# Edge masks of a sliding-window attention kernel, built by few wide operations ahead of all else

## The chip, the cores and the metric

One core of a Trainium2 chip runs the whole program. The metric is the device time of one execution in microseconds (us). TensorE appears in the profile as PE (matmuls) and PEld (weight loads), VectorE as DVE, ScalarE as ACT, GpSimd as POOL, and the queue that issues most DMAs as SP.

## The reference, cut to what matters

```python
# x: 2048 x 512, 32 heads of 16, window 256
mod = (silu(c) @ w_mod)                      # six vectors sa, ca, ga, sb, cb, gb
h = layernorm(x) * (1 + ca) + sa
q, k, v = split(h @ wqkv)                    # (cut)
mask = (i - j >= 0) & (i - j < 256)
o = softmax(where(mask, q @ k.T * Dh**-0.5, -1e9)) @ v
x = x + ga * (o @ wo)
# then a second layernorm and an MLP over tokens (cut)
```

The attention is banded. In the first four of eight stretches of rows, the blocks at the edges of the band are masked by adding a large negative number to the scores inside PSUM.

## The kernel before: the parts that matter

A mask is added by a matmul: a selector (edge_w, an identity for one half of the columns of each parity) times a triangle of zeros and -32768 (edge_t or edge_n). All three tensors are constants that GpSimd builds once.

```python
def emit_edges():                            # GpSimd throughout
    po.memset(tri4[:], 1.0)
    po.affine_select(out=tri4[:], ...)       # (cut) a triangle for each 32 rows
    po.memset(edge_w[:], 0.0)
    po.memset(edge_n[:], NEG)
    for q in range(4):
        rows = slice(32 * q, 32 * q + 32)
        po.tensor_copy(out=tri[rows, :], in_=tri4[rows, q, :])
        for a in range(2):
            for par in range(2):
                po.tensor_copy(out=edge_w[rows, a, par, a, :], in_=identity[rows, rows])
    for m in range(4):
        for diag, (a, b) in enumerate(((NEG, 0.0), (-NEG, NEG))):
            for dst in (edge_t[:, diag, m, :], edge_n[:, diag, m, diag, :]):
                po.tensor_scalar(out=dst, in0=tri[:], scalar1=a, scalar2=b, op0=ALU.mult, op1=ALU.add)
```

They are used in the scores of each stretch that adds its mask:

```python
te.matmul(dst, lhsT=edge_w[rows, a, :, :, :], rhs=neg, start=False, stop=True, ...)  # neg: edge_n or edge_t
```

Ahead of the first scores lies a start-up in which each engine works through a fixed list. PE's list opens with warm-up matmuls on zeros, whose result is not used:

```python
WARM = 24
def e_warm(e):
    te.matmul(box["warm"][:], lhsT=zt[:, 0:P], rhs=zt[:], start=True, stop=True)
# PE's order: 14 warm, transpose of silu, 2 warm, 32 small products with wmod (ps_fm),
#             transposes of x (psb), qkb, projections (pq), first scores
# DVE's order: statistics of x0, em, reciprocal, statistics of x1, silu, nm, sT, two normalizations (xn), ...
# GpSimd's order: clear a part of VT, emit_edges, clear a part of VT, split k into KT, ...
```

The softmax here doesn't subtract the row's maximum and nothing guards it: scores larger than these inputs give would overflow.

## Time and profile before

| | before |
|---|---|
| median (3 runs) | 267.24 us |
| span in the profile | 264.8 us |
| PE / DVE / ACT / GpSimd busy | 94 / 73 / 70 / 36% |
| masks complete / first read | 10.5 / 16.75 us |
| first statistics of x (DVE) | 2.86 us |
| silu ready / its transpose starts (PE) | 5.85 / 6.42 us |
| first scores | 16.63 us |

### The profile page before, as it was taken

The page shows a single profiled execution, that of the slowest core. Times are in us where ns is not written, and L with a number is a line of the kernel's source. Part 1 is how long each engine was busy: PE and PEld are TensorE (multiplying, and loading weights), DVE is VectorE, ACT ScalarE, POOL GpSimd, SP SyncE. Part 2 cuts the span into 40 slices and gives each one's busy share as a digit, 9 for nine tenths or more (in the row PEclk, how much of TensorE's full clock was granted, in tenths as well). Part 3 has the DMA queues.
Part 4 walks back from the last instruction along what each step waited for, and adds up shares of the span by engine and source line. Part 5 has one row for each costly group of instructions (what it writes and reads, how often), then busy time and mean ns, then how long its engine had stood idle before and what let it go on. Part 6 is the DMA issues. An engine that isn't in the chain of part 4 may idle for free.

```text
span 264.8 us, 10695 instructions
## 1 busy us (share of the span) xinstructions
PE 248.2 (94%) x4769; PEld 136.8 (52%) x4769; DVE 193.5 (73%) x435; ACT 185.4 (70%) x268; POOL 95.9 (36%) x182
## 2 busy tenths in 40 slices
PE   7898999999998988899999999999999999999993
PEld 2576667656556654455544454445444444444441
DVE  5778896777847359999948888999998730415875
ACT  3479999999999899999999999999416431000000
POOL 8755321495289945553893031440000000000000
PEclk9999999999999999999999999999999999999999
DMA  7995400000017000000014862020499800001122
GB/s 212 369 382 197 42 5 6 2 5 2 2 49 196 5 4 5 2 2 2 5 38 128 227 172 85 2 61 23 152 362 397 360 2 0 21 0 63 59 99 79
DMA packets 31599, 25.35 MB, mean 96 GB/s; under 512 B 6076, under 2 KB 29632, under 8 KB 31552
## 3 DMA queue, kind: packets, MB, share of 16 engines
q1 hardware_dynamic: 31544, 24.66, 29.5%
q8 instruction: 37, 0.61, 0.9%
q14 instruction: 10, 0.08, 0.1%
q10 hardware_dynamic: 8, 0.00, 0.0%
HBM read 22.55 MB, written 2.10 MB: 93 GB/s over the span
## 4 chain that ended last, share of the span: by engine, by line
PE 67%; ACT 19%; DVE 8%; issue 4%; POOL 0%; ACTq 0%; POOLq 0%
PE pu L194 32%; ACT et L194 15%; PE pxy L194 13%; PE psa L194 8%; PE pq L194 5%; PE pa L194 4%; PE pv L194 3%; ACT lz L194 3%; DVE st L194 2%; DVE VT L194 1%; PE pt L194 1%; DVE part L194 1%; DVE OT L194 1%; PE psb L194 1%; DVE h L194 1%
## 5 line engine op out<-in xcount | busy, mean ns | idle before, releaser
L194 ACT ACTIVATE et<-psa 128x1536 bf16<-128x1536 f32 x75 | 109.1, 1455 | 4.0 <-PE psa L194 2.1
L194 PE MATMUL pu<-hb,w1p 128*128 128x512 bf16 x224 | 53.1, 380 | 0.8 <-DVE part L194 0.8
L194 PE MATMUL pu<-guT,w 128*128 128x512 bf16 x224 | 49.0, 379 | 0.0
L194 ACT ACTIVATE et<-psb 128x512 bf16<-128x512 f32 x75 | 45.1, 601 | 0.0
L194 PE MATMUL pxy<-et,ones_bd 128*32 128x192 bf16 (+3 forms) x960 | 38.7, 233 | 0.9 <-issue 0.9
L194 PE MATMUL pxy<-et,VT 128*32 128x192 bf16 (+3 forms) x960 | 38.4, 234 | 0.9 <-DVE OT L194 0.5
L194 PEld LDWEIGHTS <-w 128*128 128x128 bf16 x224 | 21.9, 98 | 26.4
L194 PE MATMUL psa<-QT,KT 32*128 32x192 bf16 (+3 forms) x720 | 29.8, 230 | 5.6 <-ACT et L194 4.9
L194 PEld LDWEIGHTS <-w1p 128*128 128x128 bf16 x224 | 20.3, 98 | 25.5 <-issue 2.3
L194 POOL TENSOR_SCALAR KT<-kb,mask_par 128x512 bf16<-128x512 bf16 (+1 forms) x36 | 22.9, 645 | 25.9 <-DVE kb L194 22.2
L194 PE MATMUL pq<-h1T,wqkv 128*128 128x512 bf16 (+1 forms) x128 | 30.1, 355 | 0.3 <-ACT VT L194 0.3
L194 PEld LDWEIGHTS <-KT 32*128 32x128 bf16 x960 | 16.1, 92 | 26.2 <-issue 23.9
L194 PEld LDWEIGHTS <-VT 128*32 128x32 bf16 x960 | 23.6, 96 | 11.6 <-issue 10.1
L194 PE MATMUL psb<-QT,KT 32*128 32x192 bf16 (+3 forms) x240 | 29.3, 231 | 0.0
L194 DVE SCALAR_TENSOR_TENSOR o<-pu,b2FM,bc_all 128x512 f32<-128x512 f32 x16 | 11.6, 748 | 20.2 <-PE pu L194 20.0
L194 DVE TENSOR_TENSOR et<-et,maskt 128x512 bf16<-128x512 bf16 (+2 forms) x56 | 24.9, 480 | 0.6 <-ACT et L194 0.5
L194 PEld LDWEIGHTS <-ones_bd 128*32 128x32 bf16 x960 | 23.2, 97 | 1.2 <-issue 1.1
L194 DVE BATCH_NORM_STATS2 st<-x 128x6 f32<-128x512 bf16 x32 | 21.7, 680 | 1.3 <-DMA x<-in_A_x_dram 1.1
L194 DVE TENSOR_TENSOR OT<-pxy,lz 128x256 bf16<-128x256 f32 x32 | 13.4, 420 | 10.6 <-ACT lz L194 10.1
L194 PEld LDWEIGHTS <-wqkv 128*128 128x128 bf16 x192 | 14.0, 97 | 13.4 <-issue 4.8
L194 PE MATMUL pv<-wqkv,h1T 128*32 128x256 bf16 x512 | 17.9, 274 | 0.2 <-DVE VT L194 0.2
L194 PE MATMUL pa<-wod,OT 128*128 128x512 bf16 x64 | 17.3, 381 | 0.3 <-ACT part L194 0.3
(113 smaller groups left out, 358.2 us busy)
## 6 DMA issues: line engine op xcount, KB each, us to landing
w1p<-in_B_w_dram SPq DMA_DIRECT2D x14, 512.0 KB, 6.1
w<-in_B_w_dram SPq DMA_DIRECT2D x14, 512.0 KB, 8.4
wmod<-in_w_mod_dram SPq DMA_DIRECT2D x6, 512.0 KB, 5.5
x<-in_A_x_dram SPq DMA_DIRECT2D x16, 128.0 KB, 4.8
out_dram<-otile SPq DMA_DIRECT2D x16, 128.0 KB, 1.7
wqkv<-in_A_wqkv_dram SPq DMA_DIRECT2D x2, 384.0 KB, 5.4
wqkv<-in_A_wqkv_dram SPq DMA_DIRECT2D x1, 512.0 KB, 5.0
wod<-in_A_wo_dram SPq DMA_DIRECT2D x1, 512.0 KB, 8.4
```

Source lines behind the costliest of these rows:

```text
L194: ins = call(*args, **kwargs)
```

## The change

The intent is to build the masks sooner and with fewer instructions. The selector moves to DVE, one copy for both parities; the triangles are written for four blocks by one GpSimd operation; both go to the head of the lists.

```diff
+    def emit_edge_w():
+        ve.memset(edge_w[:], 0.0)
+        for q in range(4):
+            rows = slice(32 * q, 32 * q + 32)
+            for a in range(2):
+                ve.tensor_copy(out=edge_w[rows, a, :, a, :], in_=identity[rows, rows].unsqueeze(1).to_broadcast([32, 2, 32]))
...
-        po.memset(edge_w[:], 0.0)
...
-            for a in range(2):
-                for par in range(2):
-                    po.tensor_copy(out=edge_w[rows, a, par, a, :], in_=identity[rows, rows])
-        for m in range(4):
-            for diag, (a, b) in enumerate(((NEG, 0.0), (-NEG, NEG))):
-                for dst in (edge_t[:, diag, m, :], edge_n[:, diag, m, diag, :]):
-                    po.tensor_scalar(out=dst, in0=tri[:], ...)
+        tris = tri[:].unsqueeze(1).to_broadcast([P, 4, 32])
+        for diag, (a, b) in ((1, (-NEG, NEG)), (0, (NEG, 0.0))):
+            for dst in (edge_t[:, diag, :, :], edge_n[:, diag, :, diag, :]):
+                po.tensor_scalar(out=dst, in0=tris, ...)
```

The long list of the emission order is renumbered, and the two entries of the masks stand first in it. Nothing else moves.

## The prediction

> **What bounds the kernel now.** I read the page first, to see which engine is full and when. Part 1 gives each engine's busy time, its share of the span and its instructions:
>
> ```profile
> PE 248.2 (94%) x4769; PEld 136.8 (52%) x4769; DVE 193.5 (73%) x435; ACT 185.4 (70%) x268; POOL 95.9 (36%) x182
> ```
>
> PE is busy for 94% of the 264.8 us; GpSimd, from which the change takes work, for 36%. An engine that is a third busy can still hold up one moment, so the second question is who reads the three mask tensors (edge_w, edge_n, edge_t), and when. I asked the view by tile for edge_w in the first 20 us; its columns are shortest, median and longest duration in ns, then the first and last start:
>
> ```profile
> L194 PEld LDWEIGHTS <-edge_w x24: 92/93/93, 16.8 to 19.2; 32*128 32x128 bf16 x24
> L194 POOL COPY edge_w<-identity x16: 199/202/376, 4.0 to 7.1; 32x32 bf16<-32x32 bf16 x16
> ...
> who waited for it (us, times):
> ```
>
> GpSimd writes the selector between 4.0 and 7.5 us, PE loads it first at 16.75, and the list of those who waited for it is empty. The lists of edge_n and edge_t are empty too. The timeline of GpSimd shows the last write and what follows (start, duration, group, and in brackets the idle time before it):
>
> ```profile
> 10.28 0.21 POOL L194 TENSOR_SCALAR edge_n<-tri 128x32 bf16<-128x32 bf16 x1
> 10.43 0.95 POOL L194 MEMSET VT<- 128x1024 bf16 x1
> 14.95 1.39 POOL L194 TENSOR_SCALAR KT<-kb,mask_par 128x256 bf16<-128x256 bf16 x3 [3.57 <-ACT kb L194]
> ```
>
> The masks are complete at 10.49, 6.3 us before anyone wants them, and behind them GpSimd clears a block of VT and then waits 3.57 us for ACT's kb. So GpSimd's long build is off the path twice over.
>
> The third view is the chain of waits in order of time, over the first 17 us (start, duration, what):
>
> ```profile
> 1.33 5.16 PE pxy L194 x14
> 6.49 0.10 PE st_ps L194
> 6.60 0.54 PE pxy L194 x2
> 7.13 0.93 PE ps_fm L194 x32
> 8.06 0.47 PE psb L194 x8
> ```
>
> It runs over the warm-up matmuls (pxy), the small transpose of silu, the modulation products and the transposes of x, and later over DVE's statistics, KT, the projections and pv. GpSimd is nowhere in it before the first scores at 16.6.
>
> The last view is DVE's timeline, because the change puts new work there:
>
> ```profile
> 1.67 0.06 DVE L396 MEMSET bc_m<- 32x1 f32 x1
> 2.86 0.69 DVE L194 BATCH_NORM_STATS2 st<-x 128x6 f32<-128x512 bf16 x1 [1.13 <-DMA x<-in_A_x_dram]
> 3.59 0.18 DVE L194 BATCH_NORM_AGGREGATE mv<-st 128x2 f32<-128x6 f32 x1
> 3.69 0.25 DVE L194 TENSOR_SCALAR em<-em 4x128 f32<-4x128 f32 x1
> ...
> 5.60 0.25 DVE L194 TENSOR_TENSOR silu<-c,rm 4x128 bf16<-4x128 bf16 x1
> ```
>
> DVE sits idle for 1.13 us until the first block of x lands, then works without a gap until 5.97. The new work goes just into that hole.
>
> **What the Trainium skill says.** "VectorE: DVE Perf Modes", in its section on the TRN2 errata, counts an operation from SBUF to SBUF as 58 cycles at 0.96 GHz plus the elements over the mode's rate, and adds that a single operation was measured with about 150 fixed cycles. For a copy of 64 bf16 elements at four per cycle that is (58 + 16) / 0.96 = 77 ns, or (150 + 16) / 0.96 = 173 ns. The trace agrees with both in its way: DVE's copy of 4 elements to sT lasts 160 ns, but independent short operations start 100 ns apart (3.59 and 3.69 above), so their ends overlap. The same page, under "Zero memsets can be issued as uint32 (trn2)", says that clearing in 4-byte words halves the elements; the trace shows DVE clearing 512 bf16 of zt as 256 uint32 in 0.27 us, and the compiled new kernel shows edge_w cleared as 128 words.
>
> "SBUF — State Buffer", section "SBUF: two separate sides", says that DVE in a two-port mode and GpSimd take a shared port pair as an exclusive lock, the later one blocked for the other's whole instruction. The trace agrees for GpSimd: its slowest edge_w copy took 376 ns against a median of 202 while DVE normalized. In the other direction I see little: that DVE operation took 0.41 us, the median of its group being 0.406.
>
> **The change part by part.** Comparing the two compiled programs engine by engine: apart from renumbering, the emission order is the same, with two entries taken to the front. PE and ACT run the same instructions in the same order.
>
> Removed from GpSimd: the clearing of edge_w (from 3.09 to the next start at 3.34: 0.25 us); 16 copies of 32x32 into it (3.81 to 7.60 is 3.79 us for these and the four copies of tri; the first tri copy takes 3.96 - 3.81 = 0.15 to the next start, so 3.79 - 4 x 0.15 = 3.19 us); and 16 small triangle operations in 10.43 - 7.60 = 2.83 us.
>
> Added to GpSimd: four triangle operations of 128x128. From rows of the same operation, 128x32 takes 211 ns and 128x256 at least 473 ns, so 128x128 is an estimated 211 + 96 x (473 - 211) / 224 = 323 ns, less an overlap of 35 ns that the small ones show (211 ns long, 175 ns apart): 4 x 0.288 = 1.15 us. Net: -0.25 - 3.19 - 2.83 + 1.15 = **-5.1 us of GpSimd**. The build shrinks from 10.43 - 2.55 = 7.88 to about 2.8 us; it also moves ahead of the first clearing of VT, from 2.55 to about 1.66, and ends near 4.4. The two clearings of VT follow until about 6.3, and GpSimd then waits for ACT's kb about 8.6 us instead of 3.57. None of the 5.1 us is on the path: **0 us gained**.
>
> Added to DVE, between 1.67 and the first statistics: one clearing of 128 words (half of zt's 0.27, so 0.14 us) and eight copies of 32x64. The clearing can start near 1.70 and the first copy, which depends on it, near 1.88. At 100 to 130 ns from start to start (the 100 of above plus some for the elements: the copy to sT_rep moves 128 elements and lasts 217 ns, 57 more than that of 4 elements) the eight need 0.8 to 1.04 us and are through between 2.68 and 2.92. The first block of x lands at 2.86. So the statistics begin **0 to 0.1 us late**. If the copies did not overlap at all, at 190 ns each, they would end at 3.40 and the delay would be 0.54 us.
>
> What a delay costs: silu is ready at 5.85 and its transpose begins at 6.42. The list of waits puts 0.42 us of PE's loading there down to DVE, but the chain puts the warm-up matmuls there up to 6.49, and DVE had finished silu half a microsecond before. I choose the chain: about 0.5 us of slack. The other branch is the normalization of x at 6.71: ACT's rs is ready at 6.24, again 0.4 to 0.5 us early. A delay of 0.1 us vanishes in either, and one of 0.54 would leave about 0.1 us. Sum: **0 us, with at most a few tenths lost**. I take 267.2 us.
>
> **Rivals.** First: the lock bites DVE. GpSimd will be working without a gap from 1.66 to 6.3, and each of the eight copies may have to wait for a GpSimd operation of 0.2 to 0.5 us. Then the copies end at 1.88 + 8 x 0.2 = 3.5 or later, the statistics start 0.6 us or more late, and the time goes up by 0.1 to 0.5 us, to 267.3 to 267.7. For it: the lock as the skill tells it. Against it: the normalization above, which ran among GpSimd copies at its usual length.
>
> Second: a quieter GpSimd helps DVE. From 6.3 to 10.5 us the port pair is now free, where before some 25 GpSimd operations ran. DVE's work from 9.2 to 12.5 is on the chain, so any nanosecond saved counts. But the statistics there take 0.68 us, as at 14.12 and 14.89 (0.64 and 0.66), where few or none ran. I give it 0.1 to 0.2 us, to 267.0.
>
> Third: masks that are ready earlier let the first scores start earlier. They wait for projections and KT, and PE reaches them right behind the pq matmuls, so no: 0 us. A shift of some tenths at the start may also change which wait ends last in the crowded schedule behind it, by tenths in either direction.
>
> **Range and chances.** The three runs of before lie within 0.3 us. Together with the rivals (-0.3 to +0.5 us) I put the 8-in-10 range at 266.6 to 267.9. Two per cent would be 5.3 us, more than all GpSimd work removed, none of which is on the path, and far more than the DVE work added: 0.98 for within 2%, 0.01 for either side.
>
> **What would show each step.** Right: GpSimd busy near 90.8 us and DVE near 194.5; the last write of edge_t or edge_n ends near 4.4; GpSimd's wait for ACT's kb grows to about 8.6 us; the first statistics start by 3.0; silu's transpose stays near 6.4 and the first scores near 16.6. Wrong: first statistics at 3.3 or later, or single copies much longer than 0.2 us (first rival); first scores earlier than 16.4 with shorter DVE rows between 9 and 12.5 (second rival); or both kernels alike up to 20 us and apart later, which nothing here foresees.

## More of the kernel before

One more view than the prediction shows matters for the result: the timeline of PE's weight loads of before, as start, duration, group and, in brackets, the idle time before it.

```profile
4.72 0.15 PEld L194 LDWEIGHTS <-zt 128*128 128x128 bf16 x1 [0.28 <-issue]
5.15 0.15 PEld L194 LDWEIGHTS <-zt 128*128 128x128 bf16 x1 [0.27 <-issue]
5.47 0.53 PEld L194 LDWEIGHTS <-zt 128*128 128x128 bf16 x3 [0.17 <-issue]
6.42 0.09 PEld L194 LDWEIGHTS <-silu 4*128 4x128 bf16 x1 [0.42 <-DVE nm L194]
```

Each warm-up matmul has one load. Up to 5.15 the loads come 0.43 us apart, then three come within 0.53 us: PE changes to about twice its pace near 5.4. The row of the granted clock reads 9 tenths or more in every slice, the first too, and does not show this; the distance of the loads does. The clock records in the trace, from which that row is made, agree with the loads: the first of them begins at 5.34 us, at full clock, and the row counts the time ahead of it as full too.

## The result, and the profile after

The changed kernel took 267.37 us (median of 4 runs, 266.91 to 267.52), the kernel before 267.37 us with a fourth run added. A ratio in this document is the mean time of one kernel's runs over that of the other's of the same rounds, so not quite the ratio of the medians. Here it is 0.9997, with a 95% interval of 0.9979 to 1.0014. The time lies in the predicted range. The profile, however, did not do what the prediction said. Part 1 of the page after:

```profile
PE 248.8 (94%) x4769; PEld 136.8 (52%) x4769; DVE 195.5 (74%) x444; ACT 185.4 (70%) x268; POOL 91.1 (34%) x153
```

GpSimd lost 4.8 us of work, near the expected 5.1, but DVE gained 2.0 us instead of the expected 1.0. DVE's timeline after shows where:

```profile
1.78 0.17 DVE L194 MEMSET edge_w<- 128x128 uint32 x1
2.05 1.55 DVE L194 COPY edge_w<-identity 32x64 bf16<-32x64 bf16 x8
3.63 0.69 DVE L194 BATCH_NORM_STATS2 st<-x 128x6 f32<-128x512 bf16 x1
...
6.33 0.25 DVE L194 TENSOR_TENSOR silu<-c,rm 4x128 bf16<-4x128 bf16 x1
```

The eight copies took 1.55 us, and the statistics start at 3.63 instead of 2.86: **0.77 us late**, where 0 to 0.1 was predicted. In narrow windows of the same trace, the second copy and its neighbour on GpSimd stand side by side:

```profile
2.19 0.59 DVE L194 COPY edge_w<-identity 32x64 bf16<-32x64 bf16 x1
```

```profile
2.20 0.55 POOL L194 MEMSET edge_n<- 128x512 bf16 x1
```

One copy of 64 elements lasted as long as GpSimd's clearing of edge_n, while the median of the eight is 172 ns. And GpSimd's own timeline after:

```profile
2.70 0.98 POOL L194 COPY tri<-tri 32x32 bf16<-32x32 bf16 x4
...
4.80 1.84 POOL L194 MEMSET VT<- 128x1024 bf16 x2
15.30 1.39 POOL L194 TENSOR_SCALAR KT<-kb,mask_par 128x256 bf16<-128x256 bf16 x3 [8.66 <-ACT kb L194]
```

The build ends at 4.86 instead of 10.49, and GpSimd waits 8.66 us for ACT's kb instead of 3.57: all that it saved became idle time. Last, the chain of waits after:

```profile
1.33 5.66 PE pxy L194 x14
6.99 0.10 PE st_ps L194
7.09 0.54 PE pxy L194 x2
7.63 0.78 PE ps_fm L194 x32
```

It runs over the same warm-up matmuls, but they took 5.66 us instead of 5.16, so the transpose came 0.50 us later. The products ps_fm win 0.15 us of that back: they take 0.78 us in this chain and 0.93 in that of before, where their second half stood still between the loads at 7.33 and 7.50 (four later traces name the landing of wmod at this place). First scores came at 16.98 instead of 16.63, so this execution was 0.35 us later at that point, and its span is 0.4 us longer. Two causes were possible: the late DVE work, or a slower warm-up that has nothing to do with the change.

### The profile page after: what moved, and what is told of

Read it like the earlier page. It is cut to its first block, busy times and chain, and to the rows that moved or that the text cites. A ratio compares the mean times of both kernels' runs of the same rounds, so it can differ in the third digit from the quotient of the medians.

```text
span 265.2 us, 10676 instructions
## 1 busy us (share of the span) xinstructions
PE 248.8 (94%) x4769; PEld 136.8 (52%) x4769; DVE 195.5 (74%) x444; ACT 185.4 (70%) x268; POOL 91.1 (34%) x153
## 4 chain that ended last, share of the span: by engine, by line
PE 67%; ACT 19%; DVE 8%; issue 4%; POOL 0%; ACTq 0%; POOLq 0%
PE pu L194 32%; ACT et L194 16%; PE pxy L194 13%; PE psa L194 8%; PE pq L194 5%; PE pa L194 4%; PE pv L194 3%; ACT lz L194 3%; DVE st L194 2%; DVE VT L194 1%; PE pt L194 1%; DVE part L194 1%; PE psb L194 1%; DVE h L194 1%; DVE mv L194 0%
```

## The experiments

The theory (call it three gates): silu's transpose waits for whichever comes last, the warm-up matmuls or silu; then the products ps_fm wait for the landing of wmod. The late DVE work hides behind the other two. The rival says that the 0.77 us reach the end at least in part. A second question is why eight tiny copies took 1.55 us: because GpSimd blocks them, or because they are slow. again, pool_waits, sel_on_pool and sel_twice ran on one chip (before: 267.67 us, 11 runs), sel_gated, w10_before, w10_after and tri_twice on another (267.32 us, 11 runs), the last three on a third (268.08 us, 11 runs). All gave the right result.

### again: the changed kernel once more

No edit.

> The changed kernel once more, to narrow the interval and to have a second trace. Two theories of its profile, where DVE's first statistics start at 3.63 instead of 2.86 us but silu's transpose only 0.50 us later and the first scores 0.35 us later. WARM-UP: the transpose stands in PE's queue behind 14 warm-up matmuls, which took 5.66 us instead of 5.16 because PE changed from 0.43 us to 0.21 us per matmul about 1 us later in that execution; this differs from execution to execution and has nothing to do with the change, so the ratio to before is 0.999 to 1.001. DELAY: the late DVE work itself costs the 0.35 us, so the ratio is about 1.0013.

Measured: 267.88 us, ratio 0.9999 (0.9974 to 1.0023). The first statistics start at 3.63 and silu is ready at 6.58, just as in the first trace, but the transpose comes at 7.41 and the first scores at 17.48. PE's weight loads in this execution:

```profile
6.00 0.15 PEld L194 LDWEIGHTS <-zt 128*128 128x128 bf16 x1 [0.28 <-issue]
6.43 0.15 PEld L194 LDWEIGHTS <-zt 128*128 128x128 bf16 x1 [0.28 <-issue]
7.41 0.09 PEld L194 LDWEIGHTS <-silu 4*128 4x128 bf16 x1 [0.84 <-DVE nm L194]
```

The slow pace lasts past 6.43, and the 14 matmuls end near 7.5. The bracket names DVE, but DVE's last work ended at 6.65: it is the last releaser that the profile sees, and not what the engine waited for. Same kernel, same DVE times, half a microsecond between two executions: that is the warm-up. The first clock record stands at 6.36 us in the first trace and at 7.38 in this one. The Trainium skill, "TensorE: Matmul & The Clock Gate", Part 1, says that PE's clock doubles after a busy window of about 3.4 us that runs freely, so that the moment varies from run to run; it gives 426.7 and 215.7 ns as the distances of matmuls of this width. The trace agrees: 0.43 us and about 0.21.

### pool_waits: GpSimd idle while DVE copies

```diff
+        po.tensor_copy(out=tri[:, 0:2], in_=edge_w[:, 0, 0, 0, 0:2])
         po.memset(tri4[:], 1.0)
```

> The changed kernel, with one small GpSimd copy that reads the finished selector ahead of the triangles, so GpSimd does nothing while DVE copies. LOCK: in the changed kernel one DVE copy lasted 0.59 us, just as long as GpSimd's clearing of edge_n beside it, and the others went in pairs between GpSimd's copies. Without them the eight copies start 0.10 us apart, take 0.9 us instead of 1.55 and the first statistics start at 2.9 to 3.1 instead of 3.63. SIZE: the copies are slow by themselves (32 partitions, 64 elements, a broadcast source); they take 1.3 to 1.6 us and the statistics start after 3.4. GpSimd's build ends near 5.8 in both. Time as before, ratio 0.998 to 1.001, since the masks are wanted at 17.

Measured: 268.71 us, ratio 1.0034 (1.0008 to 1.0061). DVE's and GpSimd's rows:

```profile
2.06 1.07 DVE L194 COPY edge_w<-identity 32x64 bf16<-32x64 bf16 x8
3.16 0.69 DVE L194 BATCH_NORM_STATS2 st<-x 128x6 f32<-128x512 bf16 x1
```

```profile
3.19 0.18 POOL L194 COPY tri<-edge_w 128x2 bf16<-128x2 bf16 x1 [1.59 <-DVE edge_w L194]
```

With GpSimd still, the same eight copies take 1.07 us instead of 1.55. So 0.48 us of the delay were GpSimd's doing and 0.3 us (3.16 against 2.86) the copies' own. The lock theory holds, with copies a little slower (0.13 us from start to start) than I had written (0.10). That 0.13 is a mean of two distances: 0.09 us where a copy stays on the same 32 rows as the one before, and 0.17 to 0.18 where it goes on to the next 32. In one detail it was wrong: in the changed kernel the last six copies run from 2.80 to 3.60, also 0.13 us each, so GpSimd's short copies beside them cost nothing; the clearing of edge_n alone did.

But the time went up, which I had not expected. The trace shows one of the two normalizations of x lasting 1.69 us. The view by tile of that run gives shortest, median and longest in ns:

```profile
L194 DVE TENSOR_SCALAR xn<-x,mv,rs x2: 395/1040/1685, 6.8 to 8.4; 128x512 bf16<-128x512 bf16 x2
```

In before it reads 406/407/408. The delayed GpSimd list had put its two clearings of VT (0.95 us each) at 6.50 to 8.33, right beside them. In this execution wmod also landed late:

```profile
8.32 0.47 PEld L194 LDWEIGHTS <-wmod 128*128 128x128 bf16 x16 [0.91 <-DMA wmod<-in_w_mod_dram]
```

That is the third gate. The warm-up was over early here: PE waited for silu from near 6.0 on, and the transpose started at 6.41, 0.05 us after silu was ready at 6.36. The second normalization ended at 8.79 and the second half of ps_fm at 8.88, so this trace does not tell which of the two made the kernel slower.

### sel_on_pool: the selector back on GpSimd, still wide

```diff
-        ve.memset(edge_w[:], 0.0)
+        po.memset(edge_w[:], 0.0)
...
-                ve.tensor_copy(out=edge_w[...], ...)
+                po.tensor_copy(out=edge_w[...], ...)
```

> The changed kernel with the selector's eight wide copies on GpSimd, so DVE is as in the kernel before and only GpSimd's part of the change remains. The first statistics start at 2.86 again; GpSimd's build ends near 6.5 and its wait for kb is still 6 to 7 us. WARM-UP: same time as before, ratio 0.999 to 1.001, and silu's transpose between 6.4 and 7.0 as PE's warm-up decides. DELAY: 0.35 us faster than the changed kernel run beside it.

Measured: 268.82 us, ratio 1.0041 (1.0012 to 1.0070). This missed: with DVE untouched, the kernel is slower. The first statistics are back at 2.92 and silu at 5.84. The view by tile shows the same collision as in pool_waits:

```profile
L194 DVE TENSOR_SCALAR xn<-x,mv,rs x2: 395/956/1518, 7.5 to 9.0; 128x512 bf16<-128x512 bf16 x2
```

GpSimd's build lasts until 7.1 in this version, and the clearings of VT follow at 7.08 to 8.92, upon the normalizations. The two take 1.83 us together instead of 0.73, and 0.41% of 267.7 is 1.1 us: the sizes agree. At the first scores 0.79 us of it is left: they come 10.85 us behind the transpose, in the three traces of the changed kernel 10.06. One normalization lost more than the length of one clearing: it began during the first (at 7.54) and ended only behind the second (at 9.06), as in pool_waits (6.79 to 8.48, with clearings until 8.33). In the changed kernel the clearings end at 6.64 and the normalizations begin at 7.02 or later, since silu is never ready before 6.58. The change has this collision behind it, by starting early.

### sel_gated: the same, with the clearings of VT held back

```diff
+        if n == 0:
+            po.tensor_copy(out=VT[r][:, 0, 0, 0:2], in_=box["xn", 0, 1][:, 0:2])
         (ve if e == "DVE" else po).memset(VT[r][...], 0.0)
```

> As sel_on_pool (selector by eight wide copies on GpSimd), which was slower by 0.41% with one normalization of x stretched from 0.41 to 1.5 us while GpSimd cleared VT; but the two clearings of VT now wait for the normalized x, by a tiny GpSimd copy that reads it. COLLISION: both normalizations take 0.40 to 0.42 us again, the first scores come 1.0 to 1.1 us earlier relative to silu's transpose than in sel_on_pool, and the ratio to before is 0.998 to 1.001. If sel_on_pool was slow for another reason (masks ready later, GpSimd busier), this one stays at 1.003 to 1.005.

Measured: 268.3 us, ratio 1.0033 (1.0006 to 1.0060). Half a miss. The normalizations take 0.73 us for both again, as expected, but the time is not back. DVE's timeline tells why:

```profile
6.98 0.73 DVE L194 TENSOR_SCALAR xn<-x,mv,rs 128x512 bf16<-128x512 bf16 x2
7.82 0.16 DVE L194 COPY modFM<-ps_fm 128x4 f32<-128x4 f32 x1
8.01 0.98 DVE L194 CAST sa<-modFM 128x4 bf16<-128x4 f32 x1
9.03 0.17 DVE L194 TENSOR_TENSOR sa<-modFM,sa 128x4 bf16<-128x4 f32 x1
```

The clearings now run from 8.02 to 9.89, and a cast of four elements per row, 0.17 us in before, lasts 0.98. It lies on the chain, so 0.8 us are lost, and 0.33% of 267.3 is 0.9. The first scores come 10.69 us behind the transpose, only 0.16 us less than in sel_on_pool, where I had written 1.0 to 1.1. The time alone therefore does not rule out that the later masks or the busier GpSimd cost something; that it is the collision is read from the two traces. The cast, which began together with the first clearing (8.01 and 8.02), waited for that one alone. The copy from PSUM just ahead of it (modFM, 0.16 us) ends before the clearings begin; the statistics of x1 and silu, which in the changed kernel run beside the clearings, keep their 0.62 and 0.25 us.

### sel_twice: the suspected delay doubled

```diff
+        for _ in range(2):
             ve.memset(edge_w[:], 0.0)
             ...                                # the eight copies, inside the loop
```

> The changed kernel with the selector built twice on DVE, which doubles the suspected delay. The first statistics start near 4.8 instead of 2.86, silu is ready near 7.8, past the end of the warm-up matmuls (6.5 to 7.0 us), so silu's transpose comes at 7.9 to 8.2. WARM-UP: what lies beyond the slack is lost: 1.0 to 1.4 us later than the changed kernel at the transpose, and about the same at the first scores (17.9 to 18.4 us) and at the end, ratio 1.003 to 1.005. If delays at the start are swallowed further on (by DMA landings or other engines), the end moves by less than 0.3 us, ratio under 1.001.

Measured: 270.21 us, ratio 1.0091 (1.0062 to 1.0119), which is 2.4 us. The statistics start at 5.87, not 4.8: the second set of copies took 1.94 us, two of them 1.11 us together, beside a clearing of VT. Silu is ready at 8.79, the transpose starts at 8.83, the first scores at 19.56, which is 2.1 to 2.9 us later than in the three traces of the changed kernel (16.70 to 17.48). So in this run a delay that outgrows the gates arrives at the end in full; nothing further on swallows it. PE, idle for 2.3 us, also fell back to its slow pace: the granted clock reads 0.50 from 10 to 13 us, and the eight transposes of x took 0.88 us instead of 0.47. It cost more than I had written for both reasons: the second set of copies was longer, and from the transpose to the first scores it took 10.73 us instead of 10.06.

### w10_before and w10_after: fewer warm-up matmuls ahead of silu

```diff
-        te.matmul(box["warm"][:], ...)
+        if n not in (0, 2, 4, 19):
+            te.matmul(box["warm"][:], ...)
```

> The kernel before with 10 warm-up matmuls ahead of silu's transpose instead of 14 (even at 0.43 us each they end near 5.7), so the transpose waits for silu and no longer for the warm-up. WARM-UP: silu is ready at 5.85 and the transpose starts 0.05 us behind it, near 5.9 (6.4 to 7.4 in the traces so far). What follows waits for sT or for the landing of wmod, seen between 7 and 8.3. Time as before or a few tenths less, ratio 0.997 to 1.001; but if PE stays slow (0.43 us per matmul) for lack of warm-up, up to 0.5 us more.

> The changed kernel with the same 10 warm-up matmuls. WARM-UP: nothing hides the late DVE work now, so silu is ready at 6.58 as in both traces of the changed kernel and the transpose starts near 6.63, 0.7 us later than in w10_before. At the first scores and at the end 0.7 us remain of it if nothing else is in the way, 0 to 0.4 us if wmod lands late. If instead the late DVE work never mattered for another reason, the transposes of both start together.

Measured: w10_before 267.31 us, ratio 1.0010 (0.9983 to 1.0036); w10_after 267.77 us, ratio 1.0021 (0.9995 to 1.0047). Silu's load in each trace, before's version first:

```profile
5.91 0.09 PEld L194 LDWEIGHTS <-silu 4*128 4x128 bf16 x1 [1.30 <-DVE silu L194]
```

```profile
6.64 0.10 PEld L194 LDWEIGHTS <-silu 4*128 4x128 bf16 x1 [1.77 <-DVE silu L194]
```

With the first gate out of the way, the transposes stand 0.73 us apart, as expected, each 0.05 us behind its silu, and the first scores come at 17.18 and 17.87, 0.69 us apart. So the late DVE work is real, and in the executions where the warm-up ends last it is hidden by it. That the distance is still there at the first scores is partly chance: behind the transpose the two kernels are held up by different things, and for about the same time (11.27 and 11.23 us to the first scores). The times differ by 0.11%, 0.3 us, which the intervals do not separate. Neither kernel gained from fewer warm-up matmuls: PE was slow again or for longer (in w10_before the granted clock reads 0.50 from 8 to 11 us, and in w10_after the first clock record stands at 13.74), and in w10_before the second half of ps_fm waited for wmod until 7.36.

### tri_twice: more GpSimd work in the kernel before

```diff
-        for m in range(4):
+        for m in (0, 1, 2, 3, 0, 1, 2, 3):
```

> The kernel before with GpSimd's 16 triangle operations done twice: 2.8 us more GpSimd work, a little over half of what the change removes. OFF THE PATH: the build ends near 13.3, GpSimd's wait for ACT's kb shrinks from 3.57 to 0.7 us, the first scores stay where the warm-up puts them, ratio 0.999 to 1.001. ON THE PATH: 2.8 us of GpSimd work show up, ratio near 1.010.

Measured: 266.83 us, ratio 0.9987 (0.9964 to 1.0010). The first scores come at 16.88, and GpSimd still waits for kb:

```profile
15.19 1.39 POOL L194 TENSOR_SCALAR KT<-kb,mask_par 128x256 bf16<-128x256 bf16 x3 [1.12 <-ACT kb L194]
```

More than half of what the change takes from GpSimd, added instead, costs nothing that can be seen.

### again2, sel_on_act and act_mpar: the change a third time, and two versions out of the way of the lock

```diff
# sel_on_act: the selector's copies on ACT, behind its first exponential
-        ve.memset(edge_w[:], 0.0)
+        po.memset(edge_w[:], 0.0)
...
-                ve.tensor_copy(out=edge_w[...], in_=...)
+                ac.activation(out=edge_w[...], in_=..., func=ACT.Copy)
# act_mpar: as sel_on_act, and the entry "mpar" (two reductions on DVE) moved to the head of the order
```

> The changed kernel a third time, to narrow its ratio to before. HIDDEN: the first statistics start at 3.63, silu is ready at 6.58, and the time is that of before: 0.999 to 1.002. A small loss is left wherever the warm-up of before would have ended ahead of 6.6, so up to 0.3 us (0.1%).

> The changed kernel with the selector's eight copies on ACT, behind its first exponential, where ACT sat idle for 3.2 us, and the clearing of edge_w on GpSimd: DVE is undisturbed[...]. LOCK: the eight copies take 1.6 to 2.2 us without one of them stretched by GpSimd's clearing of edge_n, end by 4.8, ahead of ACT's rs at 5.7; the first statistics start at 2.8 to 2.95 and silu is ready near 5.85, as before the change. GpSimd's clearings of VT end near 6.6, so a normalization can be touched by 0.3 us at most. HIDDEN: no gain in time that can be told from noise, ratio 0.998 to 1.001.

> As sel_on_act, and DVE's two reductions for mask_par, 0.23 us of the chain at 10 to 11 us in every trace, moved into DVE's empty stretch ahead of the first statistics. They fit (0.31 us in a hole of 1.1), so the first statistics stay at 2.8 to 2.95 and, relative to the second qkb, KT starts 0.2 us sooner unless the pq matmuls or ACT's h1p, which run up to the same moment, hold it. Ratio to before 0.997 to 1.000; against sel_on_act 0.0 to 0.2 us faster.

**again2**: 267.52 us, ratio 0.9981 (0.9963 to 0.9999). The warm-up was over early in this trace, and the bracket names the gate rightly this time:

```profile
4.72 1.05 PEld L194 LDWEIGHTS <-zt 128*128 128x128 bf16 x5 [0.28 <-issue]
6.63 0.09 PEld L194 LDWEIGHTS <-silu 4*128 4x128 bf16 x1 [0.87 <-DVE silu L194]
```

So here the late DVE work did hold PE up: where the warm-up decides, silu's load starts 0.42 us behind the last warm-up load (in before 6.00 and 6.42), which here would have been 5.77 + 0.42 = 6.19 instead of 6.63. Yet the first scores came at 16.70, 0.07 us after the trace of before, which had lost 0.15 us at ps_fm. The time shows no loss in any of the three comparisons of the changed kernel.

**sel_on_act**: 268.37 us, ratio 1.0020 (0.9986 to 1.0054), with one run at 270.88. The mechanism is as expected: the eight copies take 1.62 us on ACT, 236 to 256 ns each, none stretched beside GpSimd; the first statistics are at 2.83, silu at 5.75, the transpose at 5.80. One normalization met the end of the clearings (they last until 6.88) and took 0.84 us, 0.44 more than undisturbed, where I had allowed 0.3; it was over at 7.03, so the other ended at 7.34. The third gate closes later still:

```profile
5.80 0.09 PEld L194 LDWEIGHTS <-silu 4*128 4x128 bf16 x1 [0.46 <-DVE silu L194]
...
7.51 0.17 PEld L194 LDWEIGHTS <-wmod 128*128 128x128 bf16 x4 [0.71 <-DMA wmod<-in_w_mod_dram]
```

The first scores come at 16.63, to the hundredth where before had them with a transpose 0.62 us later. Removing the delay altogether gains nothing at that point.

**act_mpar**: 267.91 us, ratio 0.9989 (0.9969 to 1.0008). The hole ahead of the statistics now holds work that was on the chain: from the second qkb operation to KT it takes 2.00 us (9.56 to 11.56), in all twelve other traces 2.26. That is the 0.2 us expected, and it is too small to be told in the time. No version beats before and after by more than the noise.

## Why the prediction was right

The time was right, and so were the two steps that carry it. **The removed GpSimd work is off the path**: shown by the wait for kb, 8.66 us (8.6 was written), and by tri_twice. **The score matmuls wait for nothing of the masks**: in the changed kernel, as in before, the view by tile lists no one waiting for edge_w in the first 20 us. The third rival was rightly given 0.

**The step that failed is the term "the statistics begin 0 to 0.1 us late".** It measured 0.77. Of it 0.3 us is not the lock: eight copies take 1.07 us undisturbed (pool_waits), 0.13 us from start to start, where I had taken 0.10 to 0.13; the larger part is that the first starts at 2.06 and not at 1.88. Of the two estimates for the duration of one, 77 and 173 ns, the second fits: undisturbed they last 161 to 177 ns. (The copy of 160 ns that I had set beside them, sT from st_ps, reads PSUM and is no test of figures for SBUF.) The other 0.48 us is the lock, which I had as the first rival with "0.6 us or more" of delay, and gave no share in the sum because a normalization among GpSimd's copies kept its length. That argument compared the wrong neighbour: those copies took 0.2 us each, while clearings of 0.5 and 0.95 us held the port for all their length in these traces. The first rival's mechanism was therefore right, except that one copy waited and not each of the eight, and its cost of 0.1 to 0.5 us was not seen in the time.

**The slack was read rightly from the chain, but as a constant, which it is not.** "About 0.5 us" is what the warm-up left in that execution. Where the warm-up was the later gate, the transpose started between 6.42 and 7.41 (seven of the 13 traces); silu of the changed kernel allows 6.63. Behind either, wmod can be last, and the prediction did not have this gate: in pool_waits, w10_before, sel_on_act and act_mpar the second half of ps_fm waited for it, until 7.4 to 8.3, and in before itself it stood still for 0.15 us, until 7.50. So a delay of 0.77 us, larger than the stated slack, need not reach the time; of the three traces of the changed kernel, two had the warm-up last and one silu. That the time shows nothing is partly luck, since the prediction had counted on a delay of 0.1 us at most, and a loss of a few tenths in some executions would be lost in the noise.

**"The first scores near 16.6"** failed in the profile (16.98) for the warm-up: it put the transpose 0.50 us later, and 0.15 us of this came back at ps_fm. Of the three traces of the changed kernel, one was at 16.70. **The end of the build "near 4.4"** came at 4.86, because the four tri copies in a row took 0.98 us and not 4 x 0.15. They take 0.94 to 1.07 us in every version that has them in a row, also beside DVE work that left their neighbours alone. I had sized them from the distance of two copies on the same 32 rows; these go to new rows each time, and then the next start is 0.24 us away. The trace of before has that distance too, where the rows change (an edge_w copy at 4.41, the next tri copy at 4.65). **The second rival**, a quieter GpSimd that speeds up DVE between 9 and 12.5 us, is refuted: from the second qkb to KT it takes 2.26 us before and after.

What stays open: from the first scores to the end of the span the 13 traces differ by 1.9 us (248.1 to 250.0), with no order that follows the edits. It is larger than the distance at the first scores between before and the changed kernel (0.07 to 0.85 us), and nothing here tells what makes it. The three ratios of the changed kernel to before (0.9997, 0.9999, 0.9981) show no loss, but a loss or gain of some tenths of a microsecond can't be excluded.

## What to carry to other kernels

Work moved off an idle engine gains nothing, and where it lands it must be priced with its neighbours: here a DVE copy or cast between SBUF tensors that met a long GpSimd clearing took as long as the clearing, however small it was (0.59 us beside 0.55, 0.98 beside 0.95), and one that met two clearings in a row could wait for both. Before counting on an early start, look at where the long clearings will then lie, and at all the gates of the start-up in several executions; one trace shows only the gate that was last that time. An empty stretch is best filled with work that stands on the chain later, as with mask_par here.

## What the Trainium skill lacked or had wrong

- "SBUF — State Buffer", section "Who interferes with whom": the lock is as the page says, and these runs show its size for small work, which the page lacks: a cast of 4 elements per row went from 0.17 to 0.98 us, a normalization of 512 from 0.41 to 1.52 and 1.69, all beside GpSimd clearings of 0.95 us, which read nothing. The page gives the loser's wait as the other instruction; in the last two cases it was two instructions, since the second clearing came in ahead of the waiting normalization. That bn_stats (0.62 us) and silu's two-input product (0.25 us) were untouched beside the same clearings agrees with its rules.
- "TensorE: Matmul & The Clock Gate", Part 1: the moment of the doubled pace varied more here than the 500 ns either way that it names in one place: the last load at the slow distance lies at 3.87 us in one trace (sel_on_act) and at 6.43 in another (again), and the first clock records of these two at 4.00 and 7.38. The page says elsewhere that the count of slow matmuls varies.
- No page that I read says that the trace's clock records begin only at the first change, so that the profile's row of the granted clock leaves the warm-up out: it read 9 tenths or more in every slice of both kernels. A later fall is in it: in w10_before and sel_twice the second slice reads 7.
- No page that I read gives what a change of rows costs ACT and GpSimd in a run of small copies. From start to start, on the same 32 rows and on to the next 32: ACT 0.15 to 0.16 and 0.25 us (sel_on_act), GpSimd 0.17 to 0.18 and 0.27 (64 elements, sel_on_pool).
